# A local-attention and gated-MLP kernel on one core: the order of the first transfers, products of ones on TensorE in the first unit's attention, and the placing of weight decoding

## The chip, the cores and the metric

The program runs on one NeuronCore of one Trainium2 chip. The metric is the device time of one execution, in microseconds (us). Before the change the median of 3 runs is 1194.5 us (1193.76 to 1195.43).

## The reference

The inputs are q, k and v of 8 batches x 8 heads x 576 positions x 64, and the weights of a gated MLP: w_gate and w_val (512 x 1536), w_out (1536 x 512) and a gain rms_g (512).

```python
scores = scale * q @ k.T                       # scale = 1/sqrt(64), all float32
mask   = 0 <= i - j < 32                       # heads 0 to 3
mask   = 0 <= i - j < 128 and (i - j) % 4 == 0 # heads 4 to 7
attn   = exp(scores - max) / (sum + 1e-9)      # masked positions at -1e9
x      = (attn @ v), heads side by side        # 4608 tokens x 512
xn     = x / sqrt(mean(x*x) + 1e-6) * rms_g
out    = (silu(xn @ w_gate) * (xn @ w_val)) @ w_out
```

So a query sees at most 32 keys. The kernel works in float32, either exactly or as sums of float32r parts (a high and a low part of each operand, three products).

## The kernel before

**Units.** The 4608 tokens are cut into 16 units of 288 tokens (half a batch). A unit's attention has 4 pairs of heads (c = 0 to 3) and 14 blocks of queries ("bursts"): 3 blocks of 96 queries in pairs 0 and 1, and 4 blocks of 72 queries in pairs 2 and 3, where the positions are sorted by their class modulo 4. A unit's MLP has 12 slices j of 128 hidden columns, with three parts each: the gate product (`gate`), the value product (`val`) and the output product of the slice before (`proj`).

**The order of the work.** Every engine's instruction order is written out by hand. Time is a counter `now`; `later(dt, rank, fn)` puts work off to a later tick, and `flush` issues a tick's work by rising rank. The first 25 ticks (called steps 0 to 24 here) hold nothing but the attention of unit 0, the start of its first MLP slice and the first decoding; after them come ticks with one MLP part each ("parts"), 36 for every unit, with the next unit's attention spread over them. The parts are counted from unit 0's first; the first two of them lie in step 24.

**A burst.** In step n TensorE makes the scores of burst n of unit 0 (L417, two heads, float32). VectorE adds the mask and takes the maximum one step later (L312), ScalarE the exponential two steps later (L322), VectorE the reciprocal of the sum and GpSimd the normalization three steps later (L329 to L332). TensorE transposes the result in step n+4 (LAG, L394), ScalarE copies it out of PSUM (`pt`, L374) in step n+5, and TensorE multiplies by v in step n+6 (LAG + OUT, L403). `take` (L347) brings the product to SBUF, on ScalarE and VectorE in turn. A pair's last block is followed by its squares (ScalarE L355), the multiplication by rms_g (GpSimd L357) and the sum of squares (L361). Step 22 holds `rms_sum` (L458), step 23 `rms_apply` (L500): the sum of squares over the 512 columns (rps), its root on VectorE and GpSimd (rst), a diagonal matrix (rd), and the product that spreads it over the partitions (bps). ScalarE copies that out as `root` (L505). The first products with w_gate and w_val are started in steps 19 to 23 (FIRST), before the root is known.

**The first loads.** `load(u, h)` fetches one head of units 0 and 1: with the even head the pair's q (144 KB in one transfer, L207), then a k tile whose other 64 partitions are set to zero (L211, VectorE for unit 0, GpSimd for unit 1) and whose own 64 are loaded (L212), and with the odd head the pair's v (L218). Unit 0's pairs 0 and 2 are issued by the SP queue, pairs 1 and 3 and the gain rms_g by ScalarE's queue. The q transfer's source is `qk_in[u, h:h + 2, :D, :U]`, two heads of 64 rows each. Unit 1's loads follow in steps 15, 19 and 23 and four ticks later. A transfer that comes later in the program waits for the landing of an earlier one whose semaphore it takes over; eight semaphores go round.

**Weights.** The 36 pieces of 128 x 512 (gate, value, output by slice) arrive as float64, 512 KB each, into NRAW = 4 buffers (`load_piece`, L124, SP queue), four of them ahead of step 0. Each is decoded on the chip to float32: `rebase` on ScalarE (L135), then `shift`, `low` and `sign` on VectorE (L139, L142, L146). `STEPS[n]` says how many of these VectorE operations step n issues; from part 2 on it is three for each part, until all 108 are done. `ahead` issues the rebase of a piece one or two pieces before its turn. After `sign` a piece's buffer is free and the next `load_piece` is issued. Unit 0 multiplies with the float32 pieces (L540); meanwhile `split_weight` makes the high and low parts for the units after it.

```python
STEPS = (0,) * 5 + (1,) + (2,) * 11 + (1, 1, 0, 0, 0, 1, 1, 1)   # 28 operations
def ahead():
    n = state["rebased"]
    if ops and n <= ops[0][1] + 1 and n in raws:
        rebase(n)
```

The operations stand in the order shift 0, low 0, shift 1, sign 0, low 1, shift 2, sign 1, and so on.

Of the kernel before, what the change touches and what calls it, by code (L numbers as in the profile page):

```python
# [9 lines left out]
F32 = mybir.dt.float32  # L10
BF16 = mybir.dt.bfloat16
F32R = mybir.dt.float32r
U32 = mybir.dt.uint32
AF = mybir.ActivationFunctionType
ALU = mybir.AluOpType
PSUM = bass.MemoryType.PSUM

B, H, S, D = 8, 8, 576, 64
DM, FF = 512, 1536
NT = B * S  # L20
P = 128
U = S // 2
# [4 lines left out]
NC = DM // P  # L27
NJ = FF // P
NNAT = 2
NRAW = 4  # L30
KW = DIL * (U // DIL + W)
BIG = -8e9

LAG, OUT, LATER = 4, 2, 1
STEPS = (0,) * 5 + (1,) + (2,) * 11 + (1, 1, 0, 0, 0, 1, 1, 1)
SPLITS = 30
FIRST = {19: (("g", 0), ("g", 1)), 20: (("g", 2),), 22: (("g", 3), ("v", 0), ("v", 1)),
         23: (("v", 2), ("v", 3))}  # L40

# [18 lines left out]
def attn_moe(ctx: ExitStack, tc: tile.TileContext, qk_in, v_in, w_gate, w_val, w_out, rms_g, outT):  # L60
# [37 lines left out]
    def later(dt, rank, fn):  # L98
        put_off.setdefault(now[0] + dt, []).append((rank, fn))
# [16 lines left out]
    def load_piece():  # L116
        n = state["loaded"]
        if n == len(pieces):
            return
        state["loaded"] += 1  # L120
        kind, j = pieces[n]
        raw = wp.tile([P, NC, P, 2], U32, tag="raw", name=f"raw_{kind}{j}", bufs=NRAW)
        src = {"g": w_gate, "v": w_val, "o": w_out}[kind][j]
        nc.sync.dma_start(out=raw.rearrange("p c f t -> p (c f t)"), in_=src)  # L124
        raws[n] = raw
# [48 lines left out]
# [3 lines that stand above are left out]
            rebase(n)  # L177
            state["rebased"] += 1

    def split_weight(kind, j, e):  # L180
        f = fs.pop((kind, j))
        hi = cst.tile([P, NC, P], F32R, tag=f"hi{pieces.index((kind, j))}", name=f"hi_{kind}{j}")
        lo = cst.tile([P, NC, P], F32R, tag=f"slot{state['free']}", name=f"lo_{kind}{j}")
        state["free"] = pieces.index((kind, j))
        wts[kind, j] = hi, lo
        A.copy(out=hi, in_=f)
        e.tensor_tensor(out=lo, in0=f, in1=hi, op=ALU.subtract)


    heads, vs, late = {}, {}, []  # L190

    def load(u, h):


        c, a = divmod(h, 2)
        _, _, nkt = geometry(u, c)
        if u >= NNAT:
            raw = sb.tile([P, U + KW], F32, tag="qk", name=f"qk_{u}_{h}", bufs=2)
            nc.sync.dma_start(out=raw[:, :U + nkt], in_=qk_in[u, h][:, :U + nkt])
            heads[u, h] = raw  # L200
            return
        n = 4 * (u * NC + c)
        queue = A if u == 0 and c % 2 else nc.sync
        own, other = (slice(D), slice(D, P)) if a == 0 else (slice(D, P), slice(D))
        if a == 0:
            q = cst.tile([P, U], F32, tag=f"hi{n}", name=f"q_{u}_{c}")
            queue.dma_start(out=q, in_=qk_in[u, h:h + 2, :D, :U])  # L207
        else:
            q = heads[u, h - 1][0]
        k = cst.tile([P, KW], F32, tag=f"hi{n + 1 + a}", name=f"k_{u}_{h}")  # L210
        (G if u else V).memset(k[other, :nkt], 0.0)  # L211
        queue.dma_start(out=k[own, :nkt], in_=qk_in[u, h][own, U:U + nkt])  # L212
        heads[u, h] = q, k
        if a:
            blocks, _, _ = geometry(u, c)
            rows, cols = max(b[3] for b in blocks), len(blocks) * 2 * D
            vt = cst.tile([P, DIL, 2, D], F32, tag=f"hi{n + 3}", name=f"v_{u}_{c}")
            queue.dma_start(out=vt[:rows].rearrange("p i a d -> p (i a d)")[:, :cols],  # L218
                              in_=v_in[u, c][:rows, :cols])
            for i in range(len(blocks)):  # L220
                vs[u, c, i] = vt[:, i]
# [103 lines left out]
    def scores_norm(u, c, i):  # L325
        blocks, nq, _ = geometry(u, c)
        n = blocks[i][3]
        t, sm = st[u, c, i]
        V.tensor_scalar(out=sm[:nq, 2:4], in0=sm[:nq, 2:4], scalar1=1e-9, scalar2=None, op0=ALU.add)  # L329
        V.reciprocal(out=sm[:nq, 2:4], in_=sm[:nq, 2:4])  # L330
        for a in range(2):
            G.tensor_scalar(out=t[:nq, a, :n], in0=t[:nq, a, :n], scalar1=sm[:nq, 2 + a:3 + a],  # L332
                            scalar2=1.0, op0=ALU.mult, op1=ALU.mult)

    def take(u, c, i, o):

# [299 lines left out]

    nb = len(bursts(0))
    ctx.enter_context(tc.manual_schedule())
    for h in range(H):
        load(0, h)  # L640
    A.dma_start(out=gs, in_=rms_g.rearrange("(c p) -> p c", p=P))
    for n in range(NRAW):
        load_piece()
    for h in range(H):
        later(15 + 4 * (h // 2), 9, lambda h=h: load(1, h))

    events = {}

# [25 lines left out]
    for n in range(ends):  # L674
        decode(STEPS[n])
        flush()
        t_ps = None
        if "t" in events.get(n, {}):
            t_ps = ps.tile([P, 512], F32, tag="gv"[n % 2], name=f"t_first_{n}")[:, :2 * QB]
        attend(t_ps, s_tag=("s", "acc0", "acc1", "acc3")[n % (4 if n < nb else 2)], o_tag=("o", "acc2")[n % 2])  # L680
        for kind, c in FIRST.get(n, ()):
            start(kind, c)
        if n == ends - 1:
            _, v_free = gate(0, 0), val(0, 0)
        now[0] += 1
# [100 lines left out]
```

## Time and profile before

| what | value |
|---|---|
| median of 3 runs | 1194.5 us |
| the profiled execution's own time | 1192.86 us |
| its span, first to last instruction | 1190.7 us |
| outside the span | 2.16 us |
| TensorE busy | 1140.4 us (96%) |
| VectorE, ScalarE, GpSimd busy | 755.1, 676.4, 640.8 us |
| 28 operations of decoding before part 2 | steps 5 to 24 |

The profile is of one execution. A row of the view by stretches gives the busy time of each engine in a stretch of the span with the number of instructions, the granted TensorE clock as a share of full speed, the mean busy share of the core's 16 DMA engines, and what they moved. A row of the timeline gives an instruction, or several equal ones merged ("x6"), with its start, its length and, in square brackets, the idle time before it and what ended it. PE is TensorE, DVE is VectorE, ACT ScalarE, POOL GpSimd; ACTq and SPq are the queues in which these engines issue transfers. A float32 matmul stands in two records.

### The profile page before, as it was taken

To read this page: it belongs to the slowest core of one execution; us is meant where nothing else is said; L and a number is where in the kernel's file an instruction comes from. 1 tells how busy PE (TensorE), PEld (TensorE's weight loads), DVE (VectorE), ACT (ScalarE), POOL (GpSimd) and SP (SyncE) were. 2 spreads that over 40 slices of the span, in tenths; PEclk is the share of its full clock that TensorE was granted. 3 is DMA by queue.
4 is the path that set the end of the run, shared out by engine and by line. 5 is a ranking of instruction groups with operands and counts; after the bars stand their busy time and mean duration, and the time that the engine had idled before them with its cause. 6 is when DMAs were issued, how large, how long until landed. Compare 5 with 4: busy or idle time off the path is not lost.

```text
span 1190.7 us, 26009 instructions
## 1 busy us (share of the span) xinstructions
PE 1140.4 (96%) x8492; PEld 1103.2 (93%) x8492; DVE 755.1 (63%) x2715; ACT 676.4 (57%) x2456; POOL 640.8 (54%) x1094
## 2 busy tenths in 40 slices
PE   4788899999999999999999999999999999999998
PEld 3566688999999999999999999999999999999998
DVE  4789786765658576665857656585765757575321
ACT  4567576564646556474656646465665646565221
POOL 2666476664646555464655655465555645565211
PEclk9999899999999999999999999999999999999999
DMA  4555321121213112121312212131221213120000
GB/s 151 188 186 188 106 82 50 58 80 32 77 38 92 45 51 80 35 81 36 90 40 70 68 30 78 38 101 38 68 61 35 81 37 93 40 77 16 1 21 20
DMA packets 62711, 82.19 MB, mean 69 GB/s; under 512 B 7442, under 2 KB 43282, under 8 KB 62578
## 3 DMA queue, kind: packets, MB, share of 16 engines
q1 hardware_dynamic: 61242, 79.60, 21.9%
q8 instruction: 68, 1.11, 0.4%
q10 hardware_dynamic: 1336, 0.94, 0.3%
q14 instruction: 65, 0.53, 0.1%
HBM read 71.08 MB, written 9.44 MB: 68 GB/s over the span
## 4 chain that ended last, share of the span: by engine, by line
PE 78%; DVE 14%; DMA 2%; ACT 2%; issue 2%; POOL 1%; SPq 0%; POOLq 0%; DVEq 0%
PE acc L543 8%; PE acc L544 7%; PE acc L545 7%; PE v L543 7%; PE g L543 7%; PE v L544 7%; PE v L545 7%; PE g L544 7%; PE g L545 7%; PE s L420 3%; DVE qs L290 3%; PE g L394 2%; PE o L408 2%; PE o L409 2%; DVE xraw L514 2%
## 5 line engine op out<-in xcount | busy, mean ns | idle before, releaser
L607 POOL TENSOR_TENSOR hlo<-th,hhi 128x288 fp32r<-128x288 f32 x180 | 145.4, 808 | 218.3 <-ACT hhi L606 214.2
L332 POOL TENSOR_SCALAR t<-t,sm 96x128 f32<-96x128 f32 (+3 forms) x448 | 185.2, 425 | 99.4 <-DVE sm L330 74.1
L543 PE MATMUL v<-xhi,hi_v 128*128 128x288 f32 x720 | 220.3, 306 | 3.5 <-DVE pl L378 3.2
L543 PE MATMUL acc<-hhi,hi_o 128*128 128x288 f32 x720 | 221.1, 307 | 0.0
L543 PE MATMUL g<-xhi,hi_g 128*128 128x288 f32 x720 | 219.8, 305 | 0.0
L544 PE MATMUL acc<-hlo,hi_o 128*128 128x288 f32 x720 | 212.8, 295 | 0.2 <-POOL hlo L607 0.2
L544 PE MATMUL g<-xlo,hi_g 128*128 128x288 f32 x720 | 212.9, 296 | 0.0
L544 PE MATMUL v<-xlo,hi_v 128*128 128x288 f32 x720 | 212.8, 296 | 0.0
L545 PE MATMUL acc<-hhi,lo_o 128*128 128x288 f32 x720 | 212.6, 295 | 0.0
L545 PE MATMUL g<-xhi,lo_g 128*128 128x288 f32 x720 | 212.6, 295 | 0.0
L545 PE MATMUL v<-xhi,lo_v 128*128 128x288 f32 x720 | 212.3, 295 | 0.0
L322 ACT ACTIVATE t<-t,sm 96x128 f32<-96x128 f32 (+3 forms) x448 | 166.7, 375 | 18.4 <-DMA k<-in_qk_dram 13.6
L251 POOL TENSOR_TENSOR vlo<-vt,vhi 128x128 fp32r<-128x128 f32 x196 | 98.5, 502 | 125.2 <-ACT vhi L247 109.3
L577 ACT ACTIVATE th<-g 128x288 f32<-128x288 f32 x180 | 74.0, 411 | 157.7 <-PE g L545 106.2
L606 ACT CAST hhi<-th 128x288 fp32r<-128x288 f32 x180 | 78.0, 433 | 141.2 <-DVE th L595 137.2
L543 PEld LDWEIGHTS v<-xhi,hi_v 128*128 128x128 f32 x720 | 135.3, 188 | 6.5 <-DVE pl L378 6.5
L307 DVE TENSOR_TENSOR t<-s,mask 96x256 f32<-96x256 f32 (+3 forms) x196 | 72.0, 367 | 106.7 <-PE s L420 101.1
L544 PEld LDWEIGHTS acc<-hlo,hi_o 128*128 128x128 f32 x720 | 135.8, 189 | 0.5 <-POOL hlo L607 0.5
L544 PEld LDWEIGHTS g<-xlo,hi_g 128*128 128x128 f32 x720 | 135.7, 188 | 0.1
L544 PEld LDWEIGHTS v<-xlo,hi_v 128*128 128x128 f32 x720 | 135.7, 188 | 0.0
L543 PEld LDWEIGHTS acc<-hhi,hi_o 128*128 128x128 f32 x720 | 135.5, 188 | 0.0
L543 PEld LDWEIGHTS g<-xhi,hi_g 128*128 128x128 f32 x720 | 135.3, 188 | 0.2 <-issue 0.2
(120 smaller groups left out, 2662.0 us busy)
## 6 DMA issues: line engine op xcount, KB each, us to landing
qk<-in_qk_dram SPq DMA_DIRECT2D x56, 288.0 KB, 2.9
vt<-in_v_dram SPq DMA_DIRECT2D x196, 64.0 KB, 1.8
qk<-in_qk_dram SPq DMA_DIRECT2D x28, 352.0 KB
out_dram<-ot SPq DMA_DIRECT2D x64, 144.0 KB, 1.9
qk<-in_qk_dram SPq DMA_DIRECT2D x28, 304.0 KB, 2.7
raw_g<-in_w_gate_dram SPq DMA_DIRECT2D x12, 512.0 KB, 3.1
raw_v<-in_w_val_dram SPq DMA_DIRECT2D x12, 512.0 KB, 4.0
raw_o<-in_w_out_dram SPq DMA_DIRECT2D x12, 512.0 KB
```

What stands on the lines that cost most here:

```text
L251: G.tensor_tensor(out=vl, in0=vs.pop(b), in1=vh, op=ALU.subtract)
L290: eq.tensor_tensor(out=qs[D:], in0=qr[D:], in1=qs[D:], op=ALU.subtract)
L307: V.tensor_tensor(out=t[:nq, :, :n], in0=sv[:nq, :, 1, :n], in1=mask[:nq, None, mc:mc + n].to_broadcast([nq, 2, n]), op=ALU.add)
L322: A.activation(out=t[:nq, a, :n], in_=t[:nq, a, :n], func=AF.Exp, scale=-1.0, bias=sm[:nq, a:a + 1], accum_out=sm[:nq, 2 + a:3 + a])
L332: G.tensor_scalar(out=t[:nq, a, :n], in0=t[:nq, a, :n], scalar1=sm[:nq, 2 + a:3 + a], scalar2=1.0, op0=ALU.mult, op1=ALU.mult)
L420: PE.matmul(sv[:nq, a, :, :n], qs[:, qc:qc + nq], ks[:, :, kc:kc + n], start=True, stop=True)
L543: PE.matmul(out, wh[:, cc, :], xh, start=start, stop=False)
L544: PE.matmul(out, wh[:, cc, :], xl, start=False, stop=False)
L545: PE.matmul(out, wl[:, cc, :], xh, start=False, stop=stop)
L577: A.activation(out=t, in_=g, func=AF.Tanh, scale=0.5)
L606: A.copy(out=hi, in_=t)
L607: G.tensor_tensor(out=lo, in0=t, in1=hi, op=ALU.subtract)
```

## The change

It does six things:

1. All loads of units 0 and 1 are issued by the SP queue, in the order `ORDER`: pairs 0 and 1 of unit 0, a weight piece, pair 2, a piece, pair 3, the gain, two pieces, then unit 1's pairs 0 to 3 with a piece after each of the first two. ScalarE issues no transfer.
2. The zeros of all 16 k tiles are written ahead of the loads (`zeros`), unit 1's on GpSimd as before.
3. NRAW goes from 4 to 6; two of the six raw buffers lie in the memory of the last four high parts.
4. TensorE multiplies ones by ones (128 x 128 by 128 x 512, float32r) into the bank acc3: 7 products ahead of step 0 and 3 in each of the steps 0 to 17. The scores of unit 0 rotate over three banks and no longer over four.
5. STEPS holds 22 operations: one in each of steps 5 to 13, two in each of steps 14 to 18, and one in steps 22, 23 and 24.
6. The normalization of unit 0's last three bursts (pair 3, blocks 1 to 3) goes from GpSimd to VectorE.

```diff
--- before.py
+++ after.py
@@ -27,15 +27,18 @@
 NC = DM // P
 NJ = FF // P
 NNAT = 2
-NRAW = 4
+NRAW = 6
 KW = DIL * (U // DIL + W)
 BIG = -8e9
 
 
 
 LAG, OUT, LATER = 4, 2, 1
-STEPS = (0,) * 5 + (1,) + (2,) * 11 + (1, 1, 0, 0, 0, 1, 1, 1)
+STEPS = (0,) * 5 + (1,) * 9 + (2,) * 5 + (0, 0, 0, 1, 1, 1)
+BUSY = 7, 3
 SPLITS = 30
+ORDER = [(0, 0), (0, 1), (None, 0), (0, 2), (None, 0), (0, 3), (None, 0), (None, 0),
+         (1, 0), (None, 0), (1, 1), (None, 0), (1, 2), (1, 3)]
 FIRST = {19: (("g", 0), ("g", 1)), 20: (("g", 2),), 22: (("g", 3), ("v", 0), ("v", 1)),
          23: (("v", 2), ("v", 3))}
 
@@ -119,7 +122,10 @@
             return
         state["loaded"] += 1
         kind, j = pieces[n]
-        raw = wp.tile([P, NC, P, 2], U32, tag="raw", name=f"raw_{kind}{j}", bufs=NRAW)
+        if n % NRAW < 2:
+            raw = cst.tile([P, NC, P, 2], U32, tag=f"hi{len(pieces) - 4 + 2 * (n % NRAW)}", name=f"raw_{kind}{j}")
+        else:
+            raw = wp.tile([P, NC, P, 2], U32, tag="raw", name=f"raw_{kind}{j}", bufs=NRAW - 2)
         src = {"g": w_gate, "v": w_val, "o": w_out}[kind][j]
         nc.sync.dma_start(out=raw.rearrange("p c f t -> p (c f t)"), in_=src)
         raws[n] = raw
@@ -177,17 +183,35 @@
             rebase(n)
             state["rebased"] += 1
 
+    last = {}
+
     def split_weight(kind, j, e):
         f = fs.pop((kind, j))
-        hi = cst.tile([P, NC, P], F32R, tag=f"hi{pieces.index((kind, j))}", name=f"hi_{kind}{j}")
+        n = pieces.index((kind, j))
+        if n < len(pieces) - 4:
+            hi = cst.tile([P, NC, P], F32R, tag=f"hi{n}", name=f"hi_{kind}{j}")
+        else:
+            m = n - n % 2
+            if m not in last:
+                last[m] = cst.tile([P, 2, NC, P], F32R, tag=f"hi{m}", name=f"hi_{m}")
+            hi = last[m][:, n % 2]
         lo = cst.tile([P, NC, P], F32R, tag=f"slot{state['free']}", name=f"lo_{kind}{j}")
-        state["free"] = pieces.index((kind, j))
+        state["free"] = n
         wts[kind, j] = hi, lo
         A.copy(out=hi, in_=f)
         e.tensor_tensor(out=lo, in0=f, in1=hi, op=ALU.subtract)
 
 
     heads, vs, late = {}, {}, []
+
+    zeroed = {}
+
+    def zeros(u, h):
+
+        c, a = divmod(h, 2)
+        k = cst.tile([P, KW], F32, tag=f"hi{4 * (u * NC + c) + 1 + a}", name=f"k_{u}_{h}")
+        (G if u else V).memset(k[(1 - a) * D:(2 - a) * D, :geometry(u, c)[2]], 0.0)
+        zeroed[u, h] = k
 
     def load(u, h):
 
@@ -200,22 +224,20 @@
             heads[u, h] = raw
             return
         n = 4 * (u * NC + c)
-        queue = A if u == 0 and c % 2 else nc.sync
-        own, other = (slice(D), slice(D, P)) if a == 0 else (slice(D, P), slice(D))
+        own = slice(a * D, (a + 1) * D)
         if a == 0:
             q = cst.tile([P, U], F32, tag=f"hi{n}", name=f"q_{u}_{c}")
-            queue.dma_start(out=q, in_=qk_in[u, h:h + 2, :D, :U])
+            nc.sync.dma_start(out=q, in_=qk_in[u, h:h + 2, :D, :U])
         else:
             q = heads[u, h - 1][0]
-        k = cst.tile([P, KW], F32, tag=f"hi{n + 1 + a}", name=f"k_{u}_{h}")
-        (G if u else V).memset(k[other, :nkt], 0.0)
-        queue.dma_start(out=k[own, :nkt], in_=qk_in[u, h][own, U:U + nkt])
+        k = zeroed.pop((u, h))
+        nc.sync.dma_start(out=k[own, :nkt], in_=qk_in[u, h][own, U:U + nkt])
         heads[u, h] = q, k
         if a:
             blocks, _, _ = geometry(u, c)
             rows, cols = max(b[3] for b in blocks), len(blocks) * 2 * D
             vt = cst.tile([P, DIL, 2, D], F32, tag=f"hi{n + 3}", name=f"v_{u}_{c}")
-            queue.dma_start(out=vt[:rows].rearrange("p i a d -> p (i a d)")[:, :cols],
+            nc.sync.dma_start(out=vt[:rows].rearrange("p i a d -> p (i a d)")[:, :cols],
                               in_=v_in[u, c][:rows, :cols])
             for i in range(len(blocks)):
                 vs[u, c, i] = vt[:, i]
@@ -329,8 +351,9 @@
         V.tensor_scalar(out=sm[:nq, 2:4], in0=sm[:nq, 2:4], scalar1=1e-9, scalar2=None, op0=ALU.add)
         V.reciprocal(out=sm[:nq, 2:4], in_=sm[:nq, 2:4])
         for a in range(2):
-            G.tensor_scalar(out=t[:nq, a, :n], in0=t[:nq, a, :n], scalar1=sm[:nq, 2 + a:3 + a],
-                            scalar2=1.0, op0=ALU.mult, op1=ALU.mult)
+            (V if u == 0 and (c, i) > (NC - 1, 0) else G).tensor_scalar(
+                out=t[:nq, a, :n], in0=t[:nq, a, :n], scalar1=sm[:nq, 2 + a:3 + a],
+                scalar2=1.0, op0=ALU.mult, op1=ALU.mult)
 
     def take(u, c, i, o):
 
@@ -636,13 +659,29 @@
 
     nb = len(bursts(0))
     ctx.enter_context(tc.manual_schedule())
-    for h in range(H):
-        load(0, h)
-    A.dma_start(out=gs, in_=rms_g.rearrange("(c p) -> p c", p=P))
-    for n in range(NRAW):
-        load_piece()
-    for h in range(H):
-        later(15 + 4 * (h // 2), 9, lambda h=h: load(1, h))
+    for u in range(NNAT):
+        for h in range(H):
+            zeros(u, h)
+    def load_pair(u, c):
+        for a in range(2):
+            load(u, 2 * c + a)
+
+
+    for u, c in ORDER:
+        if u is None:
+            load_piece()
+        else:
+            load_pair(u, c)
+        if (u, c) == (0, NC - 1):
+            nc.sync.dma_start(out=gs, in_=rms_g.rearrange("(c p) -> p c", p=P))
+    busy_ps = ps.tile([P, 512], F32, tag="acc3", name="busy")
+
+    def busy(n):
+
+        for _ in range(n):
+            PE.matmul(busy_ps, ones, ones[:, None, :].to_broadcast([P, 4, P]), start=True, stop=True)
+
+    busy(BUSY[0])
 
     events = {}
 
@@ -677,7 +716,9 @@
         t_ps = None
         if "t" in events.get(n, {}):
             t_ps = ps.tile([P, 512], F32, tag="gv"[n % 2], name=f"t_first_{n}")[:, :2 * QB]
-        attend(t_ps, s_tag=("s", "acc0", "acc1", "acc3")[n % (4 if n < nb else 2)], o_tag=("o", "acc2")[n % 2])
+        attend(t_ps, s_tag=("s", "acc0", "acc1")[n % (3 if n < nb else 2)], o_tag=("o", "acc2")[n % 2])
+        if n < nb + LAG:
+            busy(BUSY[1])
         for kind, c in FIRST.get(n, ()):
             start(kind, c)
         if n == ends - 1:
```

## Rows read from the trace of the kernel before

**Rows 1.** The page's first part: busy time of each engine, share, instructions.
```profile
PE 1140.4 (96%) x8492; PEld 1103.2 (93%) x8492; DVE 755.1 (63%) x2715; ACT 676.4 (57%) x2456; POOL 640.8 (54%) x1094
```

**Rows 2.** By stretches: start:end, length, busy of engines (count), clock, DMA share, GB/s.
```profile
0.00:20.00 20.00, 4.50 (x20) 3.87 (x21) 4.49 (x25) 4.04 (x15) 2.70 (x17) 1.00 0.48 144
20.00:46.00 26.00, 20.54 (x92) 16.21 (x90) 22.47 (x102) 21.38 (x84) 20.22 (x32) 1.00 0.58 198
46.00:55.50 9.50, 9.21 (x28) 7.22 (x28) 3.89 (x13) 2.19 (x5) 3.77 (x7) 1.00 0.57 176
55.50:138.50 83.00, 67.32 (x329) 51.45 (x327) 77.00 (x190) 52.49 (x157) 51.53 (x48) 0.99 0.55 177
138.50:144.00 5.50, 5.44 (x17) 4.28 (x18) 0.61 (x2) 0.27 (x1) 2.74 (x4) 0.51 0.01 5
144.00:1190.00 1046.00, 1033.38 (x8013) 1020.15 (x8011) 646.60 (x2385) 596.04 (x2196) 559.81 (x988) 1.00 0.19 55
```

**Rows 3.** Timeline of ScalarE and its transfer queue, first 56 us.
```profile
0.73 1.41 ACTq L207 DMA_DIRECT2D q<-in_qk_dram  x1
...
16.88 0.40 ACTq L641 DMA_DIRECT2D gs<-in_rms_g_dram  x1
17.34 0.37 ACT L322 ACTIVATE t<-t,sm 96x96 f32<-96x96 f32 x1 [13.57 <-DMA k<-in_qk_dram]
...
25.80 0.65 ACT L135 ACTIVATE f_o<-raw_o 128x512 f32<-128x512 f32 x1
...
45.67 0.28 ACT L374 COPY pt<-t_first 72x144 f32<-72x144 f32 x1 [1.00 <-PE o L403]
...
55.56 0.40 ACT L505 COPY root<-bps 128x288 f32<-128x288 f32 x1 [6.58 <-PE bps L500]
```

**Rows 4.** Timeline of TensorE: the first unit, and where its clock changes.
```profile
8.92 3.65 PE L417 MATMUL s<-k,q 128*96 128x96 f32 x16 [8.92 <-DMA k<-in_qk_dram]
...
46.95 3.09 PE L540 MATMUL g<-xraw,f_g 128*128 128x288 f32 x6
...
54.58 0.94 PE L500 MATMUL bps<-rd,ones 96*128 96x288 f32 x2
...
70.38 2.11 PE L540 MATMUL g<-xn,f_g 128*128 128x288 f32 x8
...
138.56 1.09 PE L458 MATMUL rps<-inv,sq 128*96 128x2 f32 x6 [4.39 <-DVE sq L361]
139.51 4.19 PE L540 MATMUL g<-xn,f_g 128*128 128x288 f32 x8
```

**Rows 5.** By stretches, columns as in rows 2: first transfers, DMA share and GB/s last.
```profile
4.00:5.00 1.00, 0.00 (x0) 0.00 (x0) 0.00 (x0) 0.00 (x0) 0.00 (x0) 1.00 0.98 308
5.00:9.00 4.00, 0.08 (x1) 0.11 (x1) 0.00 (x0) 0.00 (x0) 0.00 (x0) 1.00 0.15 52
10.99:12.00 1.01, 1.01 (x7) 0.79 (x5) 0.36 (x4) 0.00 (x0) 0.00 (x0) 1.00 0.14 49
21.00:22.00 1.00, 1.00 (x7) 1.00 (x6) 0.62 (x5) 0.71 (x2) 0.50 (x2) 1.00 1.08 398
```

**Rows 6.** Transfers by line, first 90 us: count, KB each, median us to landing.
```profile
raw_g<-in_w_gate_dram SPq DMA_DIRECT2D x8, 512.0 KB, 3.2
...
q<-in_qk_dram SPq DMA_DIRECT2D x6, 144.0 KB
```

**Rows 7.** Timeline of TensorE, steady stage: ten float32r products of 288 columns apart.
```profile
600.46 0.30 PE L544 MATMUL g<-xlo,hi_g 128*128 128x288 f32 x1
...
601.79 0.29 PE L545 MATMUL g<-xhi,lo_g 128*128 128x288 f32 x1
```

**Rows 8.** Groups of instructions by line: GpSimd's from 20 to 46 us, VectorE's from 57 to 139.
```profile
L332 POOL TENSOR_SCALAR t<-t,sm 72x72 f32<-72x72 f32 x16 | 11.4, 725 | 3.0 <-DVE sm L312 1.5 <-ACT t L322 1.4
...
L142 DVE SCALAR_TENSOR_TENSOR f_v<-raw_v,f_v 128x512 uint32<-128x512 uint32 x9 | 8.5, 944 | 0.0
...
L139 DVE TENSOR_SCALAR f_g<-f_g 128x512 uint32<-128x512 uint32 x8 | 4.1, 517 | 0.0
```

## The prediction

> **What bounds the kernel now.** The page's first part comes first: TensorE is busy for 1140.4 of 1190.7 us [rows 1]. The view by stretches says where the other 50 us are [rows 2]. From 144 us on TensorE works 1033.4 of 1046.0 us, so nothing that the change touches can shorten that stage; it only begins earlier or later. The gaps lie in front: 15.5 us up to 20 us, 5.5 in 20 to 46, 15.7 in 55.5 to 138.5. Three different limits are to be seen there. Up to 17 us it is the transfers and ScalarE's queue: ScalarE issues loads until 16.88 and makes its first exponential only at 17.34 [rows 3], though the first scores began at 8.92 [rows 4]. From 20 to 46 us VectorE (22.5 of 26) and ScalarE (21.4) are full. From 55.5 to 138.5 VectorE is: 77.0 of 83.0.
>
> The timeline of TensorE shows a fourth limit. Six records of the first gate product take 3.09 us, 0.515 each; at 70.38 eight take 2.11, 0.264 each, and at 139.51 again 0.524 [rows 4]. The granted clock of that last stretch is 0.51 [rows 2], so this is 1.2 GHz against 2.4. Before 55 us the column says 1.00, but the pace is that of 1.2 GHz; I go by the pace. The lower clock at 139 follows an idle gap of 4.39 us; TensorE works again from 138.56, and from 144 the column shows 1.00. The first unit's attention and first products thus run at half clock.
>
> **The first transfers.** A q transfer moves 144 KB [rows 6]. From 5 to 9 us, with two of them under way, the transfer engines are busy for 0.15 and move 52 GB/s; later one alone makes 0.14 and 49 GB/s; with other transfers it is 0.98 and 308, with weights 398 [rows 5]. 0.14 of 16 engines is two engines. So a q takes 147,456 B / 49 GB/s = 3.0 us on two engines whichever queue issues it, and whatever stands behind it in the one queue waits there for its share of these two. The change leaves the source of q as it is.
>
> The Trainium skill ("DMA: Bandwidth & Descriptors", on why a DMA increments its semaphore by 16) says that a transfer is spread over the largest number of engines up to 16 that divides its slowest dimension on both sides; two heads then mean two engines. The trace's 0.14 agrees, and by that rule no order of issue makes a q shorter.
>
> In rows 4 two interleaved q's end at 8.92, so data begin at about 8.92 - 2 x 3.0 = 2.9 us. The two engines then serve the new order one after another: a pair of unit 0 costs 3.0 + 1.1 us (k and v, 336 KB at 308 GB/s; 288 KB in pairs 2 and 3: 1.0), of unit 1 3.0 + 1.2 to 1.4 (352 to 416 KB), a weight piece 524,288 B / 398 GB/s = 1.3. Pair 0 has landed by 7.0 (its q and k by 6.3), pair 1 by 11.1, g0 12.4, pair 2 16.4, v0 17.7, pair 3 21.7, o0 23.0, g1 24.3; unit 1's pair 0 28.5, v1 29.8, pair 1 34.0, o1 35.3, pair 2 39.7, pair 3 44.1; and only then the seventh piece, g2: 45.4. The gain adds nothing that shows.
>
> **The attention.** The first scores start at about 6.3, not 8.92, and ScalarE is free for the exponentials at once: some 9 us are won at the first one. They are not kept. By the order of decoding, ScalarE rebases g0 and v0 in step 5, o0 in step 6, g1 in 9, v1 in 12, o1 in 14, g2 in 17 and v2 in 18. ScalarE works in order, so a rebase whose piece has not landed holds up every exponential and copy behind it. Step 6 ends with o0: 23.0 + 0.65 = 23.7, where before the same rebase stood at 25.80 (in step 7) [rows 3]. From there the steps have one operation of decoding in place of two. The stage from 20 to 46 us held some 13 steps with 21.4 us of ScalarE and 22.5 of VectorE [rows 2], 1.6 to 1.7 a step; without one operation (0.5 to 0.9 [rows 8]) VectorE is no longer the limit and ScalarE's 1.6 is. Step 17 ends at about 23.7 + 11 x 1.6 = 41.3. There g2 is awaited until 45.4, some 4 us of ScalarE standing. After it the rebase ends at 46.1 and ScalarE copies the last probabilities out; before, this copy stood at 45.67 [rows 3]. So at the end of the attention the early start is spent: +0.4 us.
>
> Normalizing three bursts on VectorE takes six operations from GpSimd at 0.73 each [rows 8]; on VectorE they fall into steps 14 to 16, ahead of that wait, and cost nothing (if the wait is gone, at most the 6 x 0.5 of its cheapest 512-column operation, 3.1; at the other end GpSimd's 4.4 saved). Unit 1's zeros go to the first 20 us, where GpSimd is busy for 2.7 [rows 2]: nothing. The bank taken from the scores: the scores of step n now wait for the maximum of step n-3, and the maximum follows its scores by a step; nothing.
>
> **The products of ones.** Ten float32r products of 288 columns lie 1.33 us apart in all [rows 7], 0.133 each; 512 columns are an estimated 0.24 us at 2.4 GHz and 0.47 at 1.2. The seven in front, 3.3 us, lie where TensorE has nothing. Three a step are 0.7 or 1.4 us. At half clock TensorE's own 20.5 us in 13 steps [rows 2] are 1.6 a step, and with 1.4 it has no idle time; this full load is what raised the clock at 46.95 to 54.58. I take it that the clock goes up in the first steps; then 0.8 + 0.7 = 1.5 a step fit beside ScalarE's 1.6.
>
> But they stop with step 17. While ScalarE waits for g2, TensorE has only the output of burst 12 left, and its next work, the output of burst 13, stands in front of the first gate products. The gap is 41.5 to 46.4, 4.9 us; the nearest row is the gap of 4.39 before 138.56, after which the clock was low until 144, 5.4 us. Before, from the gate products at 46.95 to the root's copy at 55.56 it took 8.6 us. Now they begin at 46.1 + 0.3 + 0.6 = 47.0, by the copy and the output product. At half clock throughout the root comes at 55.6 (nothing won), at full clock throughout at 47.0 + 4.3 = 51.3 (4.3 won, and the sums and roots on the other engines may not follow). I take the row: low until 46.4 + 5.4 = 51.8, and the 3.8 us left become 1.9, root at 53.7: 1.9 us won.
>
> The Trainium skill ("TensorE: Matmul & The Clock Gate", in the table on why this matters) advises against idle gaps between bursts of matmuls, since the clock falls in them; by that alone the tail would win nothing. The trace agrees with the fall, but also shows the recovery that I count.
>
> **Fewer decoding steps.** Six operations more are left for the stage that VectorE bounds. Nine groups of them stand there, from L142's at 0.94 each to L139's at 0.52 [rows 8]; all nine are 57.0 us for 81 operations, 0.70 each: 4.2 us. But every part up to part 28 issues three in both kernels; the six come in parts 29 and 30, which is the stretch from 138.5 to 144, where VectorE is busy for 0.61 of 5.5 us [rows 2]. They fit. Ends: 4.2 lost, or, if deeper prefetch lets VectorE's 6 idle us of the 83 shrink, some 3 won; I take nothing.
>
> **Sum.** 0.4 late at the copy, 1.9 won in all at the root, nothing later: 1192.86 - 1.9 = 1191.0 for the profiled execution. The median shown is 1.6 above that execution, so 1192.6.
>
> **Rivals.** (B) The weights don't hold the steps up: the two engines get through faster, or g2 is there by 41. Then the copy comes at 41.7, the clock stays up, and the root follows at 47: 8.6 us, 1186; half of it, 1189, if g2 is two us early. For it: SP no longer shares the engines with a second queue. Against it: the share of 0.14 in either case. (C) Slower by late decoding: if TensorE is not at half clock at 138.5 to 144, VectorE has no idle time there, and the six operations delay the next unit by up to 4.2 us; with nothing won at the root, 1194.5 + 4.2 = 1198.7, and with 1.9 won 1196.8. It decides as soon as VectorE is busy throughout parts 29 to 31. Against it is the idle 4.9 us. (D) The clock doesn't rise: products of ones at 1.4 a step beside 1.1 to 1.6 of its own make TensorE the bound, 45 to 54 us for 18 steps from 6.3 on, 6 to 14 us later than the copy at 45.67: 1200 to 1208. Against it is the rise at 55 under just such a load. (E) Everything hidden: 1194.5.
>
> **Chances.** A, my forecast, 0.52, with its own range 1190 to 1195.5; B 0.23; C 0.13; D 0.05; E 0.07. What a measurement here can tell from no change is 0.2%, 2.4 us. A is beyond it on the fast side in 0.22 and on the slow in 0.02, B in 0.22, C in 0.10, D in 0.05: faster 0.44, same 0.39, slower 0.17. The range runs from half of B's gain beyond 1189 to C's middle: 1187 to 1197.5.
>
> **What would show it.** In the profile after: scores from about 6.3 us and an exponential before 9; ScalarE idle behind DMA on o0 in step 6 until 23 and on g2 for 3 to 5 us until about 45; the transfer engines at a share near 0.15 for 3 us whenever a q runs alone; the first gate records partly at 0.52 and partly at 0.26; the root's copy near 53.7; the stage from 144 as before. I am wrong if g2 is not awaited, if q is spread over more engines, if the gate products run at 0.26 from the first, or if VectorE is what TensorE waits for after part 29.

## The result, and the profile after

The change makes the kernel a little slower. The median of 20 runs is 1194.72 us (1192.83 to 1196.62), against 1192.92 us (1190.31 to 1195.70) for 20 runs of the kernel before: a ratio of 1.0017 [1.0010, 1.0025]. The forecast was 1.9 us faster. The profiled execution took 1194.69 us, 2.3 us of span more than the one of before. (In the fences of the kernels after, L141, L344, L397, L426, L523, L528 and L563 are the lines that [rows 3, 4] and the text on the kernel before have as L135, L322, L374, L403, L500, L505 and L540; L682 are the products of ones.)

First the page's busy times, which answer to [rows 1]: eight us more of TensorE for 61 more records, those of the ones.

```profile
PE 1148.4 (96%) x8553; PEld 1108.6 (93%) x8553; DVE 757.7 (64%) x2721; ACT 675.6 (57%) x2456; POOL 624.0 (52%) x1088
```

The view by stretches of the kernel after, columns as in [rows 2]:

```profile
0.00:20.00 20.00, 14.49 (x70) 11.35 (x71) 7.19 (x42) 7.47 (x26) 8.10 (x29) 1.00 0.58 162
20.00:46.00 26.00, 18.21 (x104) 14.36 (x102) 17.66 (x83) 16.05 (x69) 11.61 (x19) 0.87 0.64 200
46.00:55.50 9.50, 6.24 (x22) 5.17 (x23) 3.72 (x12) 3.06 (x7) 1.37 (x3) 0.64 0.54 202
55.50:138.50 83.00, 70.76 (x334) 53.27 (x332) 77.90 (x189) 52.55 (x159) 41.59 (x47) 0.98 0.51 166
138.50:144.00 5.50, 3.05 (x11) 2.51 (x12) 5.20 (x11) 0.00 (x0) 1.43 (x2) 0.63 0.19 54
144.00:1193.00 1049.00, 1035.62 (x8019) 1021.94 (x8017) 646.01 (x2386) 596.49 (x2196) 559.91 (x990) 1.00 0.19 55
```

Much more is done before 20 us. But from 20 to 46 both ScalarE and VectorE are now far from full (16.1 and 17.7 of 26, against 21.4 and 22.5): they stand still there. The timeline of ScalarE, kernel after, says for what; it answers to [rows 3]:

```profile
8.14 0.37 ACT L344 ACTIVATE t<-t,sm 96x96 f32<-96x96 f32 x1 [5.83 <-DVE sm L334]
...
18.38 0.66 ACT L141 ACTIVATE f_v<-raw_v 128x512 f32<-128x512 f32 x1 [3.52 <-DMA raw_v<-in_w_val_dram]
...
24.50 0.66 ACT L141 ACTIVATE f_o<-raw_o 128x512 f32<-128x512 f32 x1 [4.47 <-DMA raw_o<-in_w_out_dram]
...
48.25 0.66 ACT L141 ACTIVATE f_g<-raw_g 128x512 f32<-128x512 f32 x1 [4.83 <-DMA raw_g<-in_w_gate_dram]
48.94 0.28 ACT L397 COPY pt<-t_first 72x144 f32<-72x144 f32 x1
49.49 0.68 ACT L141 ACTIVATE f_v<-raw_v 128x512 f32<-128x512 f32 x1 [0.28 <-DMA raw_v<-in_w_val_dram]
...
57.19 0.40 ACT L528 COPY root<-bps 128x288 f32<-128x288 f32 x1 [5.35 <-PE bps L523]
```

The first exponential comes 9.2 us earlier. ScalarE then waits three times for a weight piece, v0, o0 and g2, 12.8 us in all. The last copy of probabilities (pt) comes at 48.94, 3.27 us later than before. The timeline of TensorE, kernel after, shows the gap that ends with that copy and the gate products at half pace after it; it answers to [rows 4]:

```profile
44.06 0.41 PE L426 MATMUL o<-pt,v 72*128 72x144 f32 x2
49.26 0.84 PE L426 MATMUL o<-pt,v 72*128 72x144 f32 x2 [4.80 <-ACT pt L397]
49.90 3.09 PE L563 MATMUL g<-xraw,f_g 128*128 128x288 f32 x6
```

The difference of the two spans, read at the same five marks in both, is whole:

| from, to | before | after | difference |
|---|---|---|---|
| start, last copy of probabilities | 45.67 | 48.94 | +3.27 |
| copy, root | 9.89 | 8.25 | -1.64 |
| root, rps of unit 1 | 83.00 | 83.76 | +0.76 |
| rps, bps of unit 1 | 7.06 | 7.28 | +0.22 |
| that bps, end | 1045.08 | 1044.77 | -0.31 |
| sum | 1190.7 | 1193.0 | +2.30 |

Why g2 was so late begins in the queue that issues it. The timeline of SP's queue, kernel after:

```profile
30.81 0.56 SPq L230 DMA_DIRECT2D q<-in_qk_dram  x1
...
35.71 0.56 SPq L230 DMA_DIRECT2D q<-in_qk_dram  x1
36.31 2.42 SPq L234 DMA_DIRECT2D k<-in_qk_dram  x2
38.77 0.55 SPq L240 DMA_DIRECT2D v<-in_v_dram  x1
40.61 0.36 SPq L130 DMA_DIRECT2D raw_g<-in_w_gate_dram  x1
41.08 0.36 SPq L130 DMA_DIRECT2D raw_v<-in_w_val_dram  x1
41.54 0.37 SPq L130 DMA_DIRECT2D raw_o<-in_w_out_dram  x1
42.17 0.33 SPq L130 DMA_DIRECT2D raw_g<-in_w_gate_dram  x1
```

and by stretches, same kernel:

```profile
36.00:40.00 4.00, 3.50 (x22) 2.47 (x20) 3.00 (x13) 3.91 (x18) 1.58 (x3) 1.00 0.43 135
40.00:44.00 4.00, 2.67 (x14) 2.03 (x15) 3.81 (x15) 1.65 (x7) 0.48 (x1) 1.00 0.76 245
44.00:48.00 4.00, 0.46 (x3) 0.20 (x2) 1.93 (x4) 0.00 (x0) 2.02 (x2) 0.97 1.03 360
50.00:54.00 4.00, 4.00 (x14) 3.09 (x13) 1.87 (x4) 1.61 (x5) 0.78 (x1) 0.50 0.44 159
```

SP issues g2 only at 40.61, behind all of unit 1's transfers, and v2, o2 and g3 within 1.6 us of it. The buffer was not what g2 waited for. It takes over that of g0, and VectorE's timeline, same kernel, has the last operation that reads g0 done 12 us earlier:

```profile
27.80 0.68 DVE L152 SCALAR_TENSOR_TENSOR f_g<-raw_g,f_g 128x512 uint32<-128x512 uint32 x1
```

What let SP go, and why g2 still came 7.6 us later, is in the trace as well. It keeps the moments at which a transfer's semaphore is counted up, sixteen counts for a weight piece. The eighth transfer ahead of g2, whose semaphore it takes over, is pair 2's q of 30.81. The last count of this q came at 40.51, and SP issues g2 0.1 us later.

Of g2's own sixteen counts fourteen came between 43.89 and 44.47; the last two came at 47.17 and 48.23, and at 48.25 ScalarE starts. A q, which keeps 0.14 of the 16 engines busy, has just two late counts. Those of pair 3's q came at 44.30 and 45.63, those of its two k and its v behind it, the last at 45.64 and 47.21; then come g2's two, v2's (48.44 and 49.47), o2's and g3's, in the order of the queue. I read this as two engines that carry the q's and work through the queue in its order, with two of the sixteen parts of every other transfer behind them. Stretches with the share of two engines stand both ahead of the pieces and behind them:

```profile
37.50:38.50 1.00, 0.82 (x5) 0.45 (x5) 0.96 (x5) 1.00 (x5) 1.00 (x2) 1.00 0.14 50
49.50:51.00 1.50, 1.50 (x5) 1.21 (x6) 1.03 (x3) 1.28 (x4) 0.00 (x0) 0.50 0.14 57
```

So it was not the late issue that made g2 late: on these two engines pair 3 stood ahead of it until 47.21. Nor did it share the other fourteen with the pieces behind it: there g2 was done by 44.47, v2 by 45.92 and o2 by 47.43, one after another.

### The profile page after: what moved, and what is told of

Read it like the earlier page. It is cut to its first block, busy times and chain, and to the rows that moved or that the text cites. A ratio compares the mean times of both kernels' runs of the same rounds, so it can differ in the third digit from the quotient of the medians.

```text
span 1193.0 us, 26119 instructions
## 1 busy us (share of the span) xinstructions
PE 1148.4 (96%) x8553; PEld 1108.6 (93%) x8553; DVE 757.7 (64%) x2721; ACT 675.6 (57%) x2456; POOL 624.0 (52%) x1088
## 4 chain that ended last, share of the span: by engine, by line
PE 77%; DVE 16%; DMA 3%; issue 2%; ACT 1%; POOL 1%; SPq 0%; POOLq 0%; DVEq 0%
PE acc L566 8%; PE v L566 7%; PE acc L567 7%; PE acc L568 7%; PE g L566 7%; PE v L567 7%; PE v L568 7%; PE g L567 7%; PE g L568 7%; DVE qs L312 3%; PE s L443 3%; PE g L417 2%; PE o L431 2%; PE o L432 2%; DVE xraw L537 2%
## 5 line engine op out<-in xcount | busy, mean ns | idle before, releaser
L354 POOL TENSOR_SCALAR t<-t,sm 72x104 f32<-72x104 f32 (+3 forms) x442 | 169.4, 395 | 106.5 <-DVE sm L352 81.0
L566 PE MATMUL v<-xhi,hi_v 128*128 128x288 f32 x660 | 201.3, 305 | 0.9 <-DVE pl L401 0.9
L566 PE MATMUL g<-xhi,hi_g 128*128 128x288 f32 x660 | 201.0, 305 | 0.0
L567 PE MATMUL g<-xlo,hi_g 128*128 128x288 f32 x660 | 195.0, 295 | 0.0
L566 PE MATMUL acc<-hhi,hi_o 128*128 128x288 f32 x600 | 184.6, 308 | 0.0
L567 PE MATMUL acc<-hlo,hi_o 128*128 128x288 f32 x600 | 177.2, 295 | 0.0
L344 ACT ACTIVATE t<-t,sm 96x128 f32<-96x128 f32 (+3 forms) x448 | 166.7, 375 | 13.4 <-DVE sm L334 12.6
L568 PEld LDWEIGHTS acc<-hhi,lo_o 128*128 128x128 f32 x720 | 135.4, 188 | 0.0
L568 PEld LDWEIGHTS g<-xhi,lo_g 128*128 128x128 f32 x720 | 135.3, 188 | 0.0
L568 PEld LDWEIGHTS v<-xhi,lo_v 128*128 128x128 f32 x720 | 135.3, 188 | 0.0
L605 DVE SCALAR_TENSOR_TENSOR th<-th,g 128x288 f32<-128x288 f32 x180 | 80.4, 446 | 85.7 <-ACT th L600 85.2
```

What stands on the lines that cost most here:

```text
L344: A.activation(out=t[:nq, a, :n], in_=t[:nq, a, :n], func=AF.Exp, scale=-1.0, bias=sm[:nq, a:a + 1], accum_out=sm[:nq, 2 + a:3 + a])
L354: (V if u == 0 and (c, i) > (NC - 1, 0) else G).tensor_scalar(out=t[:nq, a, :n], in0=t[:nq, a, :n], scalar1=sm[:nq, 2 + a:3 + a], scalar2= ...
L566: PE.matmul(out, wh[:, cc, :], xh, start=start, stop=False)
L567: PE.matmul(out, wh[:, cc, :], xl, start=False, stop=False)
L568: PE.matmul(out, wl[:, cc, :], xh, start=False, stop=stop)
L605: V.scalar_tensor_tensor(out=t, in0=t, scalar=1.0, in1=g, op0=ALU.add, op1=ALU.mult)
```

## The experiments

Ratios are to the kernel before, run beside each. Differences between two variants are given in us by their medians; whether they can be told apart goes by these ratios.

**1. q by head, in the kernel after.**

```diff
-            nc.sync.dma_start(out=q, in_=qk_in[u, h:h + 2, :D, :U])      # with the even head
+        nc.sync.dma_start(out=q[own], in_=qk_in[u, h][own, :U])          # with each head
```

> The changed kernel with each pair's q loaded head by head, as k is, so that all 16 transfer engines take part. Theory T (the seventh weight piece stands behind unit 1's slow q transfers and holds ScalarE up): a q costs about 0.3 us of transfer time, the rebase of the seventh piece waits for nothing, the last copy of probabilities comes at 40 to 42 us instead of 48.9, the root's copy at 46 to 49 instead of 57.2, and the whole is 6 to 9 us below the changed kernel (about 1187). Rival R (the six operations of decoding moved behind the attention cost the 1.8 us): the root comes earlier all the same, but VectorE's stage then takes it up, and the whole is within 3 us of the changed kernel.

Measured: 1186.71 us, 0.9938 [0.9924, 0.9952], some 8 us faster than the change as made. A stretch of this kernel, where [rows 5] had 0.15 and 52:

```profile
5.00:9.00 4.00, 4.00 (x21) 3.34 (x20) 1.19 (x10) 1.51 (x7) 0.58 (x3) 1.00 0.70 209
```

and its ScalarE: g2's rebase waits for nothing, and pt comes 11.2 us earlier.

```profile
37.04 0.67 ACT L141 ACTIVATE f_g<-raw_g 128x512 f32<-128x512 f32 x1
37.73 0.27 ACT L397 COPY pt<-t_first 72x144 f32<-72x144 f32 x1
...
45.87 0.40 ACT L528 COPY root<-bps 128x288 f32<-128x288 f32 x1 [3.38 <-PE bps L523]
```

So the two engines of the two-head transfer were the main limit of the first 49 us: the waits for v0, o0 and g2, 12.8 us in the kernel after, are 1.97, 2.54 and 0 here. The rule of the Trainium skill that the prediction cited ("DMA: Bandwidth & Descriptors") is borne out from its other side: cut by head, the same bytes no longer hold the share at 0.15.

**2. The same edit in the kernel before.**

> The kernel before with q loaded head by head, nothing else changed. T: the first scores start at about 6 us instead of 8.9 and the exponentials some 4 us earlier; VectorE with two operations of decoding a step limits the rest, so 2 to 5 us below the kernel before (about 1189), and slower than the changed kernel with the same q by 2 to 5 us. R: faster than the changed kernel with the same q by about 1.8 us, since it has the same transfers and six operations less behind the attention.

Measured: 1187.23 us, 0.9946 [0.9934, 0.9958], 0.5 us from experiment 1 and not told apart from it. I had expected 2 to 5 us between them, and 2 to 5 us to the kernel before, where it is 5.7; the rival, faster than experiment 1 by 1.8 us, is not there either. So this expectation fell: with q cut by head, all six parts of the change together are worth nothing that these runs can measure.

**3. Unit 1's pairs out of the way.** Kernel after; its loads go back to steps 15, 19, 23 and 27, behind g2 and v2.

```diff
-         (1, 0), (None, 0), (1, 1), (None, 0), (1, 2), (1, 3)]
+         (None, 0), (None, 0)]
 ...
+    for c in range(NC):
+        later(15 + 4 * c, 9, lambda c=c: load_pair(1, c))
```

> The changed kernel with unit 1's loads where they were before, in steps 15, 19, 23 and four ticks on, and the six weight pieces directly behind unit 0's loads; q still by two heads. T: the seventh piece is issued as soon as its buffer is free and lands before step 17 ends at about 41 us; no wait of ScalarE on it, the gap of TensorE gone, root at 47 to 51 us, 4 to 8 us below the changed kernel (1187 to 1191). R: the same as the changed kernel within 1.5 us.

Measured: 1190.87 us, 0.9980 [0.9968, 0.9992], 3.9 us under the change. SP's queue in this kernel, then its ScalarE:

```profile
28.50 0.33 SPq L130 DMA_DIRECT2D raw_g<-in_w_gate_dram  x1
```

```profile
24.44 0.66 ACT L141 ACTIVATE f_o<-raw_o 128x512 f32<-128x512 f32 x1 [4.43 <-DMA raw_o<-in_w_out_dram]
...
43.33 0.67 ACT L141 ACTIVATE f_g<-raw_g 128x512 f32<-128x512 f32 x1
44.02 0.27 ACT L397 COPY pt<-t_first 72x144 f32<-72x144 f32 x1
...
52.16 0.40 ACT L528 COPY root<-bps 128x288 f32<-128x288 f32 x1 [3.38 <-PE bps L523]
```

SP issues g2 as soon as VectorE has left its buffer, and with no q ahead of it all its sixteen counts come between 31.39 and 31.65. Up to 43 us ScalarE is that of the kernel after to within 0.1 us; then the wait for g2 is gone and pt comes 4.92 earlier. The tail from copy to root takes 8.14 us here, though the clock is 1.00 from 44 to 54: without the wait TensorE stands 1.67 us for a copy of VectorE's (xraw). So the gain lies at the copy and not in the tail. The change without this queueing is a little faster than before.

**4. Without the products of ones.** Kernel after, `busy` issues nothing.

> The changed kernel without the products of ones (7 and 18 x 3 matmuls left out), all else the same. T: the wait for the seventh piece sets the end of the attention with or without them, and the clock is low there in either case, so the last copy stays near 48.9 us and the whole within 1.5 us of the changed kernel. Rival O (the products of ones hold TensorE's own work up): 2 to 4 us faster than the changed kernel.

Measured: 1194.30 us, 1.0005 [0.9997, 1.0014], not above the change with them. Its stretches:

```profile
36.00:40.00 4.00, 1.85 (x7) 1.01 (x6) 3.39 (x15) 3.85 (x18) 1.31 (x2) 0.60 0.40 120
40.00:44.00 4.00, 2.73 (x10) 1.91 (x10) 3.89 (x14) 1.37 (x5) 0.95 (x1) 0.50 0.84 234
```

The clock is at half there or nearly (0.50 to 0.60, against 1.00 with the ones), and still pt comes at 48.98, since ScalarE waits for g2 with or without them, and the root at 56.92. The ones do raise the clock; behind the gap it is at half again (0.50 from 50 to 54 with the ones, 0.51 without) when the products come that it should serve.

**5. The old 28 steps, with q by head.** Experiment 1 with the STEPS of before.

> The changed kernel with q by head and with the 28 operations of decoding. With the transfers out of the way this prices the fewer steps alone. Against the 1186.7 us with 22: the attention gets 6 x 0.65 us of VectorE more, so the root's copy moves from 45.9 to 47 to 49 us, and from the root to unit 1's sum of squares it takes 83.0 instead of 83.8 us. T: within 2 us of 1186.7. R: 2 to 4 us faster than that.

Measured: 1187.79 us, 0.9951 [0.9935, 0.9968]: 1.1 us above experiment 1, with intervals that overlap. Fewer steps neither cost nor bring what can be told here.

**6. q by head, without the ones.**

> The changed kernel with q by head and without the products of ones (all 61 matmuls left out). Transfers don't hold the attention up here. If the products of ones pay through the higher clock, TensorE's records take twice as long again in the attention and the first gate products, and the root comes 1 to 3 us later than 45.9, the whole 1 to 3 us slower than 1186.7. Rival: VectorE and ScalarE set the pace in any case and the whole stays within 1 us.

Measured: 1185.51 us, 0.9931 [0.9912, 0.9950], 1.2 us below experiment 1 and not told apart. In the profiled execution the root comes 1.9 us later than in experiment 1 (47.73 against 45.87), which the median does not bear out. Whether the ones win anything without the gap stays open.

**7. Both: q by head and unit 1 late.**

> The changed kernel with q by head and unit 1's loads in steps 15, 19, 23 and four ticks on, six weight pieces behind unit 0's loads. T: with q on all engines the order of unit 1's loads no longer matters for the seventh piece, the third piece may come a little earlier or not, and the whole is within 1.5 us of 1186.7. Rival: unit 1's transfers cost by their bytes as well and moving them gains another 1.5 to 4 us.

Measured: 1184.72 us, 0.9931 [0.9911, 0.9952]: the lowest median of all, 0.7% under the kernel before and 0.9% under the one after, though not told apart from experiments 1 and 6 (2.0 us under experiment 1, where at most 1.5 was expected). With q quick, unit 1's place in the queue brings nothing that these runs can tell.

**8. The change with the old 28 steps.** It tests the rival that the decoding's new places, and not the queue, are what the kernel after lost by.

```diff
-STEPS = (0,) * 5 + (1,) * 9 + (2,) * 5 + (0, 0, 0, 1, 1, 1)
+STEPS = (0,) * 5 + (1,) + (2,) * 11 + (1, 1, 0, 0, 0, 1, 1, 1)
```

> The changed kernel with the 28 operations of decoding in the first 25 steps that the kernel before has; two-head q and the new order as changed. Theory T (the pieces behind unit 1's transfers set the pace): the rebase of the seventh piece then stands in step 13 instead of 17 and still waits until about 48 us, four more steps of 1.6 us come after it, the last copy moves from 48.9 to 54 to 56 us, and the whole is 4 to 7 us slower than the changed kernel. Rival R (the six operations moved behind the attention cost the 1.8 us): 1 to 3 us faster than the changed kernel.

Measured: 1199.40 us, 1.0051 [1.0034, 1.0068]. ScalarE in this kernel:

```profile
38.27 0.66 ACT L141 ACTIVATE f_o<-raw_o 128x512 f32<-128x512 f32 x1 [4.62 <-DMA raw_o<-in_w_out_dram]
...
48.99 0.66 ACT L141 ACTIVATE f_g<-raw_g 128x512 f32<-128x512 f32 x1 [6.77 <-DMA raw_g<-in_w_gate_dram]
...
55.30 0.28 ACT L397 COPY pt<-t_first 72x144 f32<-72x144 f32 x1 [0.67 <-PE o L426]
```

The rival falls. The old plan asks for g2 earlier, gets it 0.7 us later (48.99 against 48.25), and has more of the attention left behind the wait. The later decoding is what keeps the loss at 0.17%.

**9. A smaller dose: only unit 1's pair 3 late.** Kernel after, pair 3 in step 27.

> The changed kernel with only unit 1's pair 3 taken out of the early queue (issued in step 27, as before); pairs 0 to 2 stay, q by two heads. Theory T: the seventh piece has one pair less in front of it (3.0 + 1.4 us by the prediction's prices) and lands at 43 to 45 us instead of 48.2; the wait of ScalarE shrinks from 4.8 to about 0 to 1.5 us, the last copy comes at 44 to 45.5, the whole is 3 to 4.5 us below the changed kernel, nearly all of what moving all four pairs gave (3.9). Rival: the piece is held up by the other weight pieces in flight with it rather than by the q transfers; it then lands less than 2 us earlier and the whole moves by less than 1.5 us.

Measured: 1190.90 us, 0.9984 [0.9973, 0.9995], the same as experiment 3. SP's queue in this kernel, then its ScalarE:

```profile
30.21 0.56 SPq L230 DMA_DIRECT2D q<-in_qk_dram  x1
...
36.03 0.34 SPq L130 DMA_DIRECT2D raw_g<-in_w_gate_dram  x1
```

```profile
44.21 0.67 ACT L141 ACTIVATE f_g<-raw_g 128x512 f32<-128x512 f32 x1
44.90 0.28 ACT L397 COPY pt<-t_first 72x144 f32<-72x144 f32 x1
```

Without pair 3 in the queue SP issues g2 4.6 us earlier. Again fourteen of its counts come together (39.55 to 40.04) and two late, at 42.96 and 44.03, 1.0 us behind the last of pair 2's v (43.03). So g2 is there 4.2 us earlier than in the kernel after, where pair 3 cost 5.1 us on the two engines, and the whole wait goes. The rival, g2 held up by the other pieces, falls. (This profiled execution is the slowest of its twelve, 1192.98 us.)

**10. Experiment 7 without the ones.**

> The changed kernel with q by head, unit 1's loads late and no products of ones, to see whether the gains add to a version below both kernels. If the two steps add: 1186.7 - 2.0 - 1.2, about 1183.5. If the products of ones are worth nothing either way: within 1 us of 1184.7, the value with them. If they pay once no transfer is waited for: 1 to 2 us above 1184.7.

Measured: 1185.86 us, 0.9943 [0.9925, 0.9961], 1.1 us above experiment 7 and not told apart.

**11. Sixteen products of ones in the gap.** Kernel after, all its waits kept; it asks what the half clock behind the gap costs.

```diff
         if n < nb + LAG:
             busy(BUSY[1])
+        elif n == nb + LAG:
+            busy(16)
```

> The changed kernel with 16 more products of ones in step 18, in the gap of 4.8 us in which TensorE waits for the last probabilities. They should keep the clock at 2.4 GHz through the first gate products. If the prediction's term for the clock is right (the tail from the last copy to the root's copy halves with the clock), the tail shrinks from 8.25 to about 5 to 6 us and the whole is 2 to 3 us below the changed kernel. Rival: the tail runs at the pace of VectorE's and ScalarE's chain (product to SBUF, squares, sum, root, spreading), as the 8.1 us at full clock with the late loads suggest; then the tail stays at 7.9 to 8.3 us and the whole within 1 us.

Measured: 1193.69 us, 0.9998 [0.9988, 1.0007], under the change's interval: 1.0 us by the medians, 0.19% by the ratios. TensorE in this kernel:

```profile
44.21 3.91 PE L682 MATMUL busy<-ones 128*128 128x512 f32 x16
49.45 0.51 PE L426 MATMUL o<-pt,v 72*128 72x144 f32 x2 [1.34 <-ACT pt L397]
49.80 1.62 PE L563 MATMUL g<-xraw,f_g 128*128 128x288 f32 x6
```

g2 is as late (48.44), and the six gate records take 1.62 us and not 3.09. From copy to root it is 6.20 us instead of 8.25: the half clock behind the gap cost 2.05. The span of this execution is only 0.7 us shorter (1192.3): from unit 1's bps to the end it takes 2.2 us more, for which see the last section. What the Trainium skill ("TensorE: Matmul & The Clock Gate") says against idle gaps holds here with that number.

## Why the prediction was wrong

**Right: the mechanism of the forecast.** Scores from 6.76 us (predicted 6.3) and an exponential at 8.14 (before 9); ScalarE behind o0 until 24.50 (23.0) and behind g2 for 4.83 us (3 to 5); a gap of TensorE of 4.80 us (4.9) with the clock at half behind it; the first gate products at half pace and later ones at full; and a q on two engines that serve the queue one transfer after another, which experiments 1 and 2 and the counts confirm. The early start was spent at the end of the attention, as said. That the wait and the gap came out so near was in part luck: both ends of the wait were over 2 us late, ScalarE's steps before it (43.42 for 41.3) and g2 (48.25 for 45.4).

Rival B (weights hold nothing up) is refuted by the waits. C (late decoding) is settled by the stretch from rps to bps of unit 1, in the kernel before and in the one after (the stretch from 138.5 to 144 cuts the kernel after 2.4 us earlier in its work, so its 5.20 us of VectorE do not compare with the 0.61 of [rows 2]):

```profile
138.56:145.62 7.06, 7.06 (x25) 5.49 (x25) 1.77 (x8) 1.89 (x6) 3.03 (x5) 0.62 0.01 2
140.95:148.23 7.28, 7.28 (x25) 5.62 (x25) 4.36 (x13) 2.10 (x7) 3.61 (x5) 0.60 0.00 0
```

VectorE works 2.6 us more there, so most of the six operations did go there, and the stretch grew by only 0.22. D is refuted by TensorE's pace in the kernel after: three products of ones take 1.63 us at first and 0.94 at 10.97, so the clock did rise in the first steps (behind the wait for o0 it falls once, to 0.50 from 24 to 30 us).

```profile
7.39 1.63 PE L682 MATMUL busy<-ones 128*128 128x512 f32 x3
...
10.97 0.94 PE L682 MATMUL busy<-ones 128*128 128x512 f32 x3
```

Later it is 1.00 from 36 to 44 us, against 0.50 to 0.60 without the ones (experiment 4).

**Wrong: the price of a pair on the two engines, and with it "and only then the seventh piece, g2: 45.4".** The chain of the forecast is found again in the last counts, link by link, and falls behind on the way:

| landed, us | predicted | last count |
|---|---|---|
| unit 0's pair 1 | 11.1 | 11.22 |
| v0 | 17.7 | 18.36 |
| o0 | 23.0 | 24.47 |
| unit 1's pair 0 | 28.5 | 29.95 |
| pair 1 | 34.0 | 36.06 |
| pair 2 | 39.7 | 42.10 |
| pair 3 | 44.1 | 47.21 |
| g2 | 45.4 | 48.23 |

g2's own step, 1.0 us behind the last pair, is no longer than the 1.3 put for it. But the six pairs behind g0, put at 4.0 to 4.4 us each and 25.2 together, took 4.1 to 5.1 and 27.3; the seven pieces took 0.6 more than their 9.1. Within the pairs it is the q: from the last count of the transfer ahead to its own, a q took 3.0 to 4.1 us, 20.9 for the six in place of 18.0 (their k and v took 0.8 less than put). The 3.0 came from a stretch with one q alone at 49 GB/s, and the two first q's, which it fits, have nothing beside them either; what makes the later ones longer stays open. Experiments 3 and 9 show that unit 1's pairs ahead of g2 are the cause: move four of them or one, and the wait is 0. Experiment 8 shows that the step which asks for g2 is not. With g2 at 45.4 the sum was -1.9; 2.8 more is +0.9, already on the wrong side.

**Smaller terms.** The tail from copy to root was put at 7.6 and took 8.25. The clock in it came back as the row had it (0.50 until 54.6, 5.3 us behind the first work after the gap, for 5.4). But from the first gate products to the root it took 7.29 us for 6.7, so against the 8.61 of before the recovery won 1.3 and not 1.9. At full clock throughout, put at 4.3, it is 5.5 (experiment 11) and 5.7 (experiment 3): as the forecast's own bracket feared, the sums and roots on the other engines don't follow. The stretch from root to unit 1's rps, put at no change, took 0.76 more. It is 83.8 to 83.9 in experiments 1, 3 to 5 and 7 as well, with 22 steps or 28, with the ones or without, so neither is the cause; what is stays open (in experiment 2, on the kernel before, it was 86.0, so the 83.0 isn't fixed either). 2.84 late at the copy, + 0.65 in the tail, + 0.76, + 0.22, - 0.31 makes 4.2 over the forecast's -1.9: the 2.3 of the spans. One sum of the rivals was off: half of B's 8.6 us leaves 1190.2 and not 1189.

**The weighing.** Against a loss stood only C and D, both about other places. A rival "g2 later than 45.4" had a place, a price (1 us for 1 us) and a reason in the sum itself: fifteen links, 42.5 us long, priced by single rows, in which an error of 5% is 2.1 us, more than the whole gain. It was missing.

## What to carry to other kernels

Before reordering a queue, look at how wide each transfer in it runs: a stretch with a share of 0.15 says that two of 16 engines work, and cutting that transfer by its outer dimension brought more (0.5 to 0.6%) than reordering (0.2% in experiments 3 and 9). A wide transfer behind narrow ones has landed only when its parts on the narrow ones' engines have: put its arrival behind all of them, whenever it is issued. A chain of many links, each priced by one row, needs an error of its own; where that is larger than the gain, a loss belongs among the rivals. Products that keep the clock up have to stand in the gap itself; ahead of it they gave nothing.

## What the runs showed of the hardware that was not expected

Behind two-engine transfers a 512 KB piece is nearly there long before it counts: fourteen of g2's sixteen counts were in at 44.47, the last at 48.23. With no q ahead of it (experiment 3) all sixteen came within 0.3 us, 3.2 us after its issue.

And the clock doesn't fall at the same place in each execution. In the profiled one of experiment 9 it is already low while the ones run. In those of experiments 1, 3 and 11 it falls once more between 185 and 205 us, where the kernels before and after show 1.00, and from unit 1's bps to the end they take 1046.9 to 1047.0 us in place of 1044.8 to 1045.1; why stays open. A stretch each of experiments 9 and 11:

```profile
40.00:44.00 4.00, 2.77 (x13) 1.46 (x11) 3.81 (x15) 2.19 (x10) 0.00 (x0) 0.80 0.79 238
195.00:205.00 10.00, 8.91 (x58) 8.81 (x59) 6.11 (x25) 6.20 (x23) 5.82 (x12) 0.83 0.19 53
```
